# Attention over a cached window with output projection: the last output block in pieces of 512, 256, 160 and 96 columns, its last store in two row halves

## The chip, the cores and the metric

The kernel runs on one core of one Trainium2 chip. The metric is device time in microseconds, the median of several executions. One more execution was recorded with the hardware profiler; durations and times within the run come from that one.

## The reference

Queries are projected from x, attend over the last 2048 positions of a key and value cache (8 query heads share each of 4 key/value heads), and the result goes through an output projection:

```python
B, Sq, D = 8, 32, 1024
Hq, Hkv, Sk, Dh = 32, 4, 8192, 128
W = min(4096, max(256, Sk // 4))
rep = Hq // Hkv
q = (x @ wq).reshape(B, Sq, Hq, Dh).transpose(0, 2, 1, 3)
k = jnp.repeat(k_cache[:, :, Sk - W:, :], rep, axis=1)
v = jnp.repeat(v_cache[:, :, Sk - W:, :], rep, axis=1)
scores = jnp.einsum("bhqd,bhkd->bhqk", q, k) * (Dh ** -0.5)
o = jnp.einsum("bhqk,bhkd->bhqd", softmax(scores), v)
out = o.transpose(0, 2, 1, 3).reshape(B, Sq, Hq * Dh) @ wo
```

Everything is bf16. The output is 256 rows (8 batches of 32 positions) by 1024 columns, 512 KB.

## The kernel before

The work is cut into 32 units, one for each pair of batch and key/value head, ordered by head (line 129). A unit has four chunks of four key blocks; each chunk is a set of score matmuls (line 504), an exponential on ScalarE (line 506) and, two chunks later, the matmuls of probabilities with values (line 515). VectorE normalizes a finished unit and turns it into OT (`finish_unit`, lines 441 to 453), the stationary operand of the output projection. Projections of queries and of outputs are cut into small pieces which `side_plan` puts between the chunks by hand-written slots, so that TensorE always has work. The order of the instructions on each engine is the order in which the program issues them (manual schedule, line 75).

`o_pieces` (line 309) makes the output projection. For one head group g and one block t of 128 output rows it goes over column pieces given by `cuts`; each piece has four parts of two matmuls (line 322), which add up in one PSUM tile. After the fourth part VectorE takes the sum out. For the first three groups it is collected in `oacc` in FP32; for the last group it is added to `oacc`, written as bf16 to an `o_t` tile (line 332) and stored (line 334). A store goes out on SyncE's queue (SP) where its first column is 0 or 768, and else on ScalarE's (ACT).

The last group of the first row block is in the plan. The last group of the second row block is the end of the kernel: `tail_begin` (line 533) finishes the last unit, counts whether all softmax sums were in range, and makes the pieces with the cuts (512, 256, 128, 128) in line 541. `tail_mid` (line 546) runs the matmuls of the first piece and the first half of the second and opens two PSUM tiles for the last two pieces, under their first columns 768 and 896. Between the two, the engines read the count and branch: a fallback with the exact maximum, which is not taken here, or `tail_end` (line 554), which does the first piece's eviction and store, the rest of the second piece, and the last two. So the last four stores are, in order: 512 columns on SP, 256 on ACT, 128 on SP, 128 on ACT, each of 128 rows, each waiting for its eviction.

At the end of the tile context, shown by the profile as line 689, SP waits for the semaphores of all DMAs, one instruction after the other, before the engines meet in a closing barrier. The DMAs of the whole program use eight completion semaphores in turn, in the order in which they are issued in the program.

Of the kernel before, what the change touches and what calls it, by code (L numbers as in the profile page):

```python
# [108 lines left out]
class Fast:  # L109
# [199 lines left out]
    def o_pieces(self, g, t, cuts=(512, 512), st=None):  # L309

        nc, P = self.nc, self.P
        st = {} if st is None else st
        last = g == self.Hkv - 1

        def piece(n0, w, i, mm=None):

            if i == 0 and n0 not in st:
                st[n0] = self.ps_m.tile([P, 512], FP32, name="op_ps", tag="m")
            ps = st[n0]
            for k in range(i * 2, i * 2 + 2) if mm is not False else ():  # L320
                gq, c = g * self.QT_N + k // 4, k % 4
                nc.tensor.matmul(ps[:, 0:w], lhsT=self.OT[:, gq, c, t * P:(t + 1) * P],  # L322
                                 rhs=self.wo_t[gq][:, c, n0:n0 + w], start=(k == 0), stop=(k == 7))
            if i == 3 and mm is not True:
                acc = self.oacc[:, t, n0:n0 + w]
                if g == 0:
                    nc.vector.tensor_copy(out=acc, in_=ps[:, 0:w])
                elif not last:
                    nc.vector.tensor_tensor(out=acc, in0=ps[:, 0:w], in1=acc, op=ALU.add)  # L329
                else:  # L330
                    o_t = self.osb.tile([P, 512], BF16, name="o_t")
                    nc.vector.tensor_tensor(out=o_t[:, 0:w], in0=ps[:, 0:w], in1=acc, op=ALU.add)  # L332
                    eng = nc.sync if n0 in (0, 768) else nc.scalar
                    eng.dma_start(out=self.out[t * P:(t + 1) * P, n0:n0 + w], in_=o_t[:, 0:w])
        return [lambda n0=sum(cuts[:k]), w=w, i=i, **kw: piece(n0, w, i, **kw) for k, w in enumerate(cuts) for i in range(4)]


# [195 lines left out]
    def tail_begin(self):  # L533
        self.pv_last()
        for p in self.after[:-2]:
            p()
        low = self.check_all()
        for p in self.after[-2:]:
            p()
        self.open = {}  # L540
        self.last = self.o_pieces(self.Hkv - 1, 1, (512, 256, 128, 128), self.open)
        for p in self.last[:2]:
            p()
        return low

    def tail_mid(self):
        self.last[2]()
        self.last[3](mm=True)
        for p in self.last[4:6]:
            p()  # L550
        for n0 in (768, 896):
            self.open[n0] = self.ps_o.tile([self.P, 512], FP32, name="op_ps", tag="o_ps")

    def tail_end(self):
# [139 lines left out]
```

## Time and profile before

| What | Value |
|---|---|
| Median of 5 runs | 184.38 us (184.13 to 186.41) |
| The profiled execution's own time | 184.45 us |
| Its span, first to last instruction | 182.7 us |
| Busy share of PE, DVE, ACT, POOL | 98%, 69%, 74%, 49% |
| Granted TensorE clock | 0.999 |
| Output matmuls (line 322) | 144, 36.2 us busy |
| Last store, issue to landing | 1.5 us |

The span is 1.8 us shorter than the execution's own time, which also holds what lies before the first and after the last instruction. PE is the matmul row, PEld the weight loads which run beside it; DVE is VectorE, ACT ScalarE, POOL GpSimd. A "q" after an engine's name is its sequencer, which issues DMAs and waits. The issue of a DMA is short; its landing comes later, and "to landing" counts from the start of the issue until the last of its semaphore's increments. The chain of waits follows the work back from the last busy instruction; it does not follow a DMA that nobody computes with, so the time after the last eviction is to be looked for in the windows and in the records of SP.

### The profile page before, as it was taken

What the parts mean: (1) busy time and instruction counts of PE and PEld (TensorE: products, weight loads), DVE (VectorE), ACT (ScalarE), POOL (GpSimd) and SP (SyncE); (2) the same over time, 40 slices, a digit from 0 to 9 for tenths busy, and PEclk for the clock granted to TensorE, in tenths of its full rate; (3) what the DMA queues carried; (4) which work ended last, traced back from release to release, by engine and by line L of the source; (5) the groups of instructions that cost most, each with busy time, mean ns of one, the idle gap of its engine ahead of it and who ended that gap; (6) DMA issues with size and microseconds to landing.
All of it is one profiled execution on the core that took longest, in us unless ns stands there. A gap on an engine that the chain in (4) does not pass through costs nothing.

```text
span 182.7 us, 5030 instructions
## 1 busy us (share of the span) xinstructions
PE 178.3 (98%) x2041; PEld 152.3 (83%) x2041; DVE 125.6 (69%) x257; ACT 135.9 (74%) x146; POOL 89.1 (49%) x138
## 2 busy tenths in 40 slices
PE   8899999999999999999999999999999999999993
PEld 3799899999999999988787899988787788888843
DVE  0238699778977698487898655967587987554253
ACT  2218898897897888997877787888878788888800
POOL 2002565069780795935949607929606959600000
PEclk9999999999999999999999999999999999999999
DMA  5999999989999999999999999999999999970013
GB/s 187 337 410 404 228 385 375 228 278 256 369 391 252 359 266 345 369 297 316 303 377 376 399 255 275 369 241 365 256 330 266 324 303 327 212 172 0 0 34 92
DMA packets 52954, 51.73 MB, mean 283 GB/s; under 512 B 39744, under 2 KB 40256, under 8 KB 52928
## 3 DMA queue, kind: packets, MB, share of 16 engines
q1 hardware_dynamic: 52352, 50.90, 98.6%
q10 hardware_dynamic: 576, 0.49, 0.8%
q8 instruction: 16, 0.26, 0.6%
q14 instruction: 10, 0.08, 0.1%
HBM read 41.42 MB, written 0.52 MB: 230 GB/s over the span
## 4 chain that ended last, share of the span: by engine, by line
PE 86%; DMA 9%; DVE 1%; SPq 1%; issue 0%
PE o_ps L515 30%; PE s_ps L504 29%; PE op_ps L322 15%; PE q_ps L285 11%; DMA k_raw<-in_k_cache_dram 9%; SPq L168 1%; PE ql_ps L301 0%; DVE kb L259 0%; DVE kT L246 0%; DVE OT L451 0%; DVE o_sb L449 0%; SPq L347 0%; DVE o_t L332 0%; PE cnt_ps L570 0%; DVE RL_all L445 0%
## 5 line engine op out<-in xcount | busy, mean ns | idle before, releaser
L506 ACT ACTIVATE pT<-s_ps 128x1024 bf16<-128x1024 f32 x128 | 128.4, 1027 | 27.2 <-PE s_ps L504 27.0
L270 POOL TENSOR_SCALAR kTv<-kb 32x512 bf16<-32x512 bf16 x126 | 84.4, 670 | 51.0 <-DVE kb L259 31.7
L515 PE MATMUL o_ps<-va,pT 128*128 128x129 bf16 x1024 | 78.8, 220 | 0.0
L515 PEld LDWEIGHTS <-pT 128*128 128x128 bf16 x1024 | 68.5, 98 | 3.1
L504 PE MATMUL s_ps<-QT,kT 128*128 128x256 bf16 x336 | 50.4, 273 | 0.2 <-DVE kT L246 0.2
L504 PEld LDWEIGHTS <-kT 128*128 128x128 bf16 x336 | 31.8, 98 | 9.8 <-DVE kT L246 0.3
L322 PE MATMUL op_ps<-wo_sb,OT 128*128 128x512 bf16 (+2 forms) x144 | 36.2, 356 | 0.0
L259 DVE STREAM_TRANSPOSE kb<-k_raw 128x512 bf16<-128x512 bf16 x44 | 29.7, 691 | 1.9 <-DMA k_raw<-in_k_cache_dram 1.5
L285 PE MATMUL q_ps<-xT,wq_sb 128*128 128x256 bf16 x192 | 28.3, 273 | 0.0
L504 PE MATMUL s_ps<-QT,kTv 128*128 128x256 bf16 x176 | 26.4, 273 | 0.0
L439 DVE COPY va<-v_sb 128x2048 bf16<-128x2048 bf16 x30 | 25.2, 841 | 1.6 <-DMA v_sb<-in_v_cache_dram 1.3
L445 DVE RECIPROCAL RL_all<-o_ps 128x2 f32<-128x2 f32 x32 | 5.3, 164 | 26.7 <-PE o_ps L515 26.4
L268 DVE COPY kTv<-kb 32x512 bf16<-32x512 bf16 x50 | 22.7, 455 | 1.2
L504 PEld LDWEIGHTS <-kTv 128*128 128x128 bf16 x176 | 17.0, 98 | 6.1
L285 PEld LDWEIGHTS <-wq_sb 128*128 128x128 bf16 x192 | 16.9, 98 | 1.2
L451 DVE STREAM_TRANSPOSE OT<-o_sb 128x256 bf16<-128x256 bf16 x32 | 14.3, 445 | 1.1
L449 DVE TENSOR_TENSOR o_sb<-o_ps,RL_all 128x256 bf16<-128x256 f32 x32 | 13.6, 424 | 1.1
L322 PEld LDWEIGHTS <-OT 128*128 128x128 bf16 x144 | 11.3, 98 | 2.3
L437 POOL TENSOR_SCALAR va<-v_sb 128x2048 bf16<-128x2048 bf16 x2 | 3.8, 1897 | 17.6 <-DMA v_sb<-in_v_cache_dram 17.6
L288 ACT CAST QT<-q_ps 128x512 bf16<-128x512 f32 x12 | 7.0, 583 | 0.2 <-PE q_ps L285 0.2
L329 DVE TENSOR_TENSOR oacc<-op_ps,oacc 128x512 f32<-128x512 f32 x8 | 5.3, 662 | 2.0 <-PE op_ps L322 2.0
L405 PE MATMUL q_ps<-xT,wq_sb 128*128 128x256 bf16 (+1 forms) x64 | 6.0, 246 | 0.7 <-DMA wq_sb<-in_wq_dram 0.5
(35 smaller groups left out, 42.5 us busy)
## 6 DMA issues: line engine op xcount, KB each, us to landing
v_sb<-in_v_cache_dram SPq DMA_DIRECT2D x30, 512.0 KB, 6.6
wo_sb<-in_wo_dram SPq DMA_DIRECT2D x16, 512.0 KB, 6.4
wq_sb<-in_wq_dram SPq DMA_DIRECT2D x13, 512.0 KB, 6.6
k_raw<-in_k_cache_dram SPq DMA_DIRECT2D x13, 512.0 KB, 5.7
wq_sb<-in_wq_dram SPq DMA_DIRECT2D x6, 256.0 KB, 5.1
v_sb<-in_v_cache_dram SPq DMA_DIRECT2D x4, 256.0 KB, 4.6
kT<-in_k_cache_dram SPq DMA_TRANSPOSE x36, 7.1
k_raw<-in_k_cache_dram SPq DMA_DIRECT2D x2, 256.0 KB, 6.4
```

Of the source, the lines that this page charges most:

```text
L259: nc.vector.transpose(out=st["kb"][:, sl, :], in_=self.k_raw[ui][:, sl, :])
L268: nc.vector.tensor_copy(out=out, in_=in_)
L270: nc.gpsimd.tensor_scalar(out=out, in0=in_, scalar1=1.0, scalar2=1.0, op0=ALU.mult, op1=ALU.mult)
L285: nc.tensor.matmul(st[k][:, hl % 2, :], lhsT=self.wq_t[g, i][:, c % (DC // 2), hl * P:(hl + 1) * P], rhs=self.xT[:, c, :], start=(c == 0 a ...
L288: nc.scalar.copy(out=self.q_view(g)[:, :, 2 * k:2 * k + 2, :].rearrange("p b h s -> p h b s"), in_=st[k][:, :, :].rearrange("p h (b s) -> ...
L322: nc.tensor.matmul(ps[:, 0:w], lhsT=self.OT[:, gq, c, t * P:(t + 1) * P], rhs=self.wo_t[gq][:, c, n0:n0 + w], start=(k == 0), stop=(k == 7))
L439: self.nc.vector.tensor_copy(out=out, in_=in_)
L449: nc.vector.tensor_tensor(out=o_sb[:, :, :, :], in0=o_ps[:, :, 0:Dh].rearrange("p q (i c) -> p q c i", c=4), in1=rl[:, ui * QT_N:(ui + 1) ...
L451: nc.vector.transpose(out=self.OT[:, g * QT_N:(g + 1) * QT_N, :, b * self.Sq:(b + 1) * self.Sq], in_=o_sb[:, :, :, :])
L504: nc.tensor.matmul(s_ps[:, jj, :], lhsT=self.kT[ui][:, c * CJ + jj, :], rhs=q_u, start=True, stop=True)
L506: nc.scalar.activation(out=pT[:, :, :], in_=s_ps[:, :, :], func=ACT.Exp, bias=0.0, scale=self.scale)
L515: nc.tensor.matmul(o_ps[:, qt, 0:self.VW], lhsT=pT[:, jj, qt * P:(qt + 1) * P], rhs=va[:, j, 0:self.VW], start=(j == 0 and qt == 0), stop= ...
```

## The change

The last two pieces are 160 and 96 columns wide instead of 128 and 128. The 256-column store moves from ACT's queue to SP's, the first of the two narrow pieces from SP's to ACT's, and the last piece is stored by two DMAs: rows 0 to 63 on SP, rows 64 to 127 on ACT.

```diff
                     nc.vector.tensor_tensor(out=o_t[:, 0:w], in0=ps[:, 0:w], in1=acc, op=ALU.add)
-                    eng = nc.sync if n0 in (0, 768) else nc.scalar
-                    eng.dma_start(out=self.out[t * P:(t + 1) * P, n0:n0 + w], in_=o_t[:, 0:w])
+                    if n0 == 928:
+                        for p0, eng in ((0, nc.sync), (P // 2, nc.scalar)):
+                            eng.dma_start(out=self.out[t * P + p0:t * P + p0 + P // 2, n0:n0 + w], in_=o_t[p0:p0 + P // 2, 0:w])
+                    else:
+                        eng = nc.sync if n0 == 0 or w == 256 else nc.scalar
+                        eng.dma_start(out=self.out[t * P:(t + 1) * P, n0:n0 + w], in_=o_t[:, 0:w])
...
-        self.last = self.o_pieces(self.Hkv - 1, 1, (512, 256, 128, 128), self.open)
+        self.last = self.o_pieces(self.Hkv - 1, 1, (512, 256, 160, 96), self.open)
...
-        for n0 in (768, 896):
+        for n0 in (768, 928):
             self.open[n0] = self.ps_o.tile([self.P, 512], FP32, name="op_ps", tag="o_ps")
```

After the change the last five stores are: 512 columns on SP, 256 on SP, 160 on ACT, and 96 columns by 64 rows on each of SP and ACT. Nothing else of the program is changed.

## The prediction

> **What bounds the kernel now.** I read the page first, then the chain of waits over the last microseconds, the groups by shape of the same stretch, a table of windows, and last the single records of the stores and of SyncE's (SP's) closing waits. The page's chain says where the whole time lies:
>
> ```profile
> PE 86%; DMA 9%; DVE 1%; SPq 1%; issue 0%
> ```
>
> TensorE sets the time nearly from end to end, and none of its earlier work is touched. So the question is only what follows the last matmuls. The chain of waits from 178 us on:
>
> ```profile
> 177.94 2.00 PE op_ps L322 x25
> 179.94 0.02 issue
> 179.96 0.29 DVE o_t L332
> ```
>
> It ends at 180.25 with VectorE's last eviction, but the span ends at 182.67: the last 2.42 us are store and closing, which the chain does not follow. The windows (columns: length, then busy time of PE, PEld, DVE, ACT, POOL with counts, then granted clock, DMA share, GB/s):
>
> ```profile
> 178.86:179.98 1.12, 1.06 (x18) 0.88 (x15) 0.83 (x4) 0.00 (x0) 0.00 (x0) 1.00 0.22 65
> 179.98:180.62 0.64, 0.00 (x0) 0.00 (x0) 0.27 (x1) 0.00 (x0) 0.00 (x0) 1.00 0.77 221
> 180.62:181.78 1.16, 0.00 (x0) 0.00 (x0) 0.00 (x0) 0.00 (x0) 0.00 (x0) 1.00 0.32 71
> 181.78:182.67 0.89, 0.00 (x0) 0.00 (x0) 0.00 (x0) 0.00 (x0) 0.00 (x0) 0.77 0.00 0
> ```
>
> The reader is to see four stages: 16 matmuls of 128 columns with evictions; the last eviction and the issue of the last store; 1.16 us of that store's flight with every compute engine idle; 0.89 us of closing barrier. The last two stores (issue times near 180 us), and SP's closing waits in two stretches:
>
> ```profile
> L334 SPq DMA_DIRECT2D out_dram<-o_t x1: 618/618/618, 179.8 to 179.8; - x1
> L334 ACTq DMA_DIRECT2D out_dram<-o_t x1: 339/339/339, 180.3 to 180.3; - x1
> DMA to landing us min/median/max: 1.5/1.6/1.8
> ...
> L689 SPq EVENT_SEMAPHORE  x4: 28/28/28, 180.5 to 180.7; - x4
> ...
> L689 SPq EVENT_SEMAPHORE  x4: 28/28/28, 181.3 to 181.8; - x4
> ```
>
> SP closes the program by waiting for the eight store and load semaphores one after the other. The first four were long complete and pass at 180.495, 180.564, 180.631 and 180.695: 67 ns apiece, the bare price of a wait. The other four are the last four stores in the order of their landing; they pass at 181.257, 181.445, 181.620 and 181.792, each about 16 ns after its store landed (the last at 181.776). So only the last landing is paid, and the seven other waits hide under it. From the eighth wait to the end it is 0.88 us.
>
> **The change, part by part.**
>
> *Matmuls.* 8 x 128 and 8 x 128 columns become 8 x 160 and 8 x 96, the same columns in all. In the records the starts are 55.8 ns apart at 128 columns, 109 at 256, 216 at 512: 2.5 ns plus columns at 2.4 per ns. So 160 columns take 69.3 ns. No matmul of 96 is in the trace: by the line through the rows 42.6 ns, and, if the 128-column weight load ahead of each (98 ns long, back to back at the same 56 ns) is as fast as it gets, 56. The Trainium skill (TensorE: Matmul & The Clock Gate, Back-to-back issue gap) has both sides: N/2.4 + 2.5 for a lone matmul, and about 81 ns at N=128 for a stream of load and matmul. This trace's 55.8 ns in such a stream speaks for the line; with a floor of 81 the last eight would end 0.31 us later. I take 42.6: the last matmul starts at 178.865 + 8 x 0.0693 + 7 x 0.0426 = 179.717 instead of 179.702; the 56 ns end adds 0.09 us and is kept for the range.
>
> *Evictions.* The shapes give VectorE's price and the matmul's latency:
>
> ```profile
> L332 DVE TENSOR_TENSOR o_t<-op_ps,oacc 128x512 bf16<-128x512 f32 x3 | 2.1, 692 | 3.8 <-PE op_ps L322 3.8
> L322 PE MATMUL op_ps<-wo_sb,OT 128*128 128x128 bf16 x16 | 1.1, 219 | 0.0
> L332 DVE TENSOR_TENSOR o_t<-op_ps,oacc 128x128 bf16<-128x128 f32 x2 | 0.6, 290 | 0.2 <-PE op_ps L322 0.2
> L332 DVE TENSOR_TENSOR o_t<-op_ps,oacc 128x256 bf16<-128x256 f32 x1 | 0.4, 425 | 0.1
> ```
>
> From 290 and 425 ns it is 1.05 ns a column: 160 columns cost 324, 96 cost 256. The eviction of 160 can start when its matmuls are out (179.35 + 0.23 + 0.04 = 179.62) and ends at 179.94; that of 96 starts 0.245 us after the last matmul's start (0.258 before, less 13 ns of shorter matmul), at 179.96, and ends at 180.22 instead of 180.25. The longer eviction is just hidden by TensorE; gain 0.03 us.
>
> *Stores that change queue.* The 256-column store goes from ACT to SP. SP's queue holds the 512 store (issued 178.98 to 179.33), so it is free at 179.52 and pays nothing. The 160-column store goes to ACT at 179.97 and holds ACT's queue for 0.34 us (339 to 356 ns in ACT's three rows), to 180.32. Neither is late for anybody but what stands behind them: ACT's half store. That one can only be issued at 180.32 plus about 0.09 for the wait and issue between two stores, some 180.41, where before the last store went out at 180.28. SP's half finds SP free and goes out at 180.25.
>
> *The split.* One store of 32 KB becomes two of 12 KB: one more issue, one more semaphore. A store's first packet comes 0.49 to 0.52 us after its issue ended in all six stores, and the last landing 0.66 us after the first packet for both 256-byte stores. Of those 0.66 us, eight packets per DMA engine of about 16 to 18 ns are 0.13; halving the rows saves about 0.06. The Trainium skill speaks against the split (DMA: Bandwidth & Descriptors, Rules for kernel authors): two transfers on disjoint partition halves serialize on the same 16 engines, so one should not bother. By that rule the saving is nothing, by the packets' row 0.06; I take 0.06, since the two are issued 0.16 us apart and each has only some 0.07 us of packets. The flight is a fixed latency in the main, which a half store pays in full. The time to issue 64 rows is in no row: 0.34 if fixed, 0.17 if it goes with the rows. I take 0.34, since 1024, 512 and 256 byte rows cost 349, 343 and 339, so it hardly follows size; SP's last issue, 618, is the upper end. Then SP's half lands at 180.25 + 0.34 + 0.50 + 0.60 = 181.69 and ACT's at 180.41 + 0.34 + 0.50 + 0.60 = 181.85, against 181.78 before.
>
> *The closing waits.* Here the change costs something that its lines don't show. The DMAs take eight semaphores in turn, and the last store of before had the eighth. The added store is therefore on the first one again, and the built program gives it to SP's half: the first of SP's eight closing waits now asks for that store's landing. The other seven, which passed under the flight before, stand behind it: 7 x 67 ns = 0.47 us. The eighth passes at 181.69 + 0.02 + 0.47 = 182.18 instead of 181.79. ACT's half, landing at 181.85, is hidden by that. Everything after (0.88 us) is the same.
>
> *Sum.* 182.18 - 181.79 = +0.39 us: matmul and eviction -0.03, halved store -0.06, closing waits +0.47, rounding +0.01. The profiled execution is 184.45 us, 1.78 more than its span, and would be 184.84. The median of the runs shown, 184.38, is 0.07 below it, so I forecast **184.77 us**, 0.2% more. A measurement of this kernel can tell about 1%, 1.8 us, from no change, so in these terms it is no change.
>
> **The rivals.**
>
> 1. *Issue time goes with the rows.* With 0.17 for a half store SP's lands at 181.52, the eighth wait passes at 182.01: +0.22, 184.60 us. For it: the descriptors are halved. Against it: the flat row above.
> 2. *SP's issue is long again.* The 618 ns row fell beside the other stores' packets, and SP's half, beside ACT's issues, may meet the same: 0.28 more, +0.67, 185.05 us. Its cause isn't in the profile, so I can't exclude it; three of four other late stores that overlap traffic or another issue kept to 0.35.
> 3. *It gains, with the end set by the landing of the last half.* With an issue of 0.17, ACT's half lands at 181.68, and if the closing waits cost nothing the end moves by -0.10: 184.28 us. The 67 ns steps at 180.5 to 180.7 speak against it, and so does the place of SP's half as the first wait.
> 4. *Slower by over 1%: small rows written badly.* The last rows are 192 bytes, starting 1856 bytes into a 2048-byte row of the output. If such a write takes much longer to be confirmed than the 256-byte one, everything waits for it. It decides from 1.84 - 0.39 = 1.45 us more, 2.1 us instead of 0.66 from first packet to landing; at that price the time is 186.2 us. Against it: packets of 1024, 512 and 256 bytes took 46, 27 and 18 ns, a smooth row, and 256 bytes showed no step.
>
> **How the numbers follow.** The forecast 0.54, rival 1 0.17, rival 2 0.16, rival 3 0.1, rival 4 0.03. The likeliest one's own range is 184.5 to 185.0. The range over all adds rival 2 with the weight-load bound on top (185.05 + 0.09) and a share of the scatter of the five runs (184.13 to 186.41, above the median more than below), and rival 3 with it below: 184.2 to 185.4. Faster by over 1% needs 1.8 us out of 2.4 that are nearly all fixed latency: 0.01. Slower by over 1% is rival 4 and a disturbed median: 0.04. Within 1%: 0.95.
>
> **What would show it.** Right: a first closing wait that passes near 181.7 and seven behind it at 67 ns steps, the eighth near 182.2; ACT's half issued near 180.4; last matmuls 43 ns apart; span near 183.1. Wrong: closing waits that end with the last landing (rival 3), an SP issue well above 0.34 (rival 2) or near 0.17 (rival 1), matmuls of 96 columns at 56 ns (0.09 more), or over a microsecond from packet to landing (rival 4).

## The result and the profile after

The changed kernel is slower by 0.42%: the ratio of its time to the kernel before is 1.0042, 95% interval 1.0028 to 1.0055. Its median is 185.5 us (42 runs) against 184.69 us for the kernel before in 79 runs. The forecast was 184.77 us, +0.39, in a range that ended at 185.4. The direction was right, the cost was twice as large, and the result lies just above the range. A part of the miss is the base: with more runs the median before moved from 184.38 to 184.69. But the difference itself, 0.8 us, is also twice the forecast.

The profiled execution took 185.34 us, its span went from 182.7 to 183.6. Of this 0.9 us, 0.21 lie ahead of everything that was changed: the eviction of the 512-column piece starts at 178.475 us instead of 178.263, with the same program up to there. Such scatter comes from run to run (over all traces of this case that start lies between 178.00 and 178.74). So all times below that are called "from the mark" are counted from the start of that eviction, in the single records of each trace. There the eighth closing wait passes at 3.53 us before and at 4.21 after: the change costs 0.68 us in the tail.

The chain of waits of the changed kernel from 178.2 us on ends in the same way as before:

```profile
178.15 2.00 PE op_ps L322 x25
180.15 0.02 issue
180.17 0.26 DVE o_t L332
```

The same 2.00 us of matmuls, and an eviction of 0.26 instead of 0.29. The windows of the changed kernel, cut at the same events as before (first of the last 16 matmuls, start of the last eviction, end of the last store's issue, 0.01 us ahead of the eighth closing wait, end; columns as in the windows of before):

```profile
179.08:180.17 1.09, 1.05 (x18) 0.91 (x15) 0.84 (x3) 0.00 (x0) 0.00 (x0) 1.00 0.15 45
180.17:181.17 1.00, 0.00 (x0) 0.00 (x0) 0.26 (x1) 0.00 (x0) 0.00 (x0) 1.00 0.62 186
181.17:182.67 1.50, 0.00 (x0) 0.00 (x0) 0.00 (x0) 0.00 (x0) 0.00 (x0) 1.00 0.17 31
182.67:183.56 0.89, 0.00 (x0) 0.00 (x0) 0.00 (x0) 0.00 (x0) 0.00 (x0) 0.62 0.00 0
```

The compute stage became no longer (1.09 for 1.12) and the closing barrier is the same (0.89). The two stages between them grew: eviction and issue from 0.64 to 1.00, flight and closing waits from 1.16 to 1.50. The shapes of the last pieces in the changed kernel:

```profile
L322 PE MATMUL op_ps<-wo_sb,OT 128*128 128x160 bf16 x8 | 0.7, 233 | 0.0
L322 PE MATMUL op_ps<-wo_sb,OT 128*128 128x96 bf16 x8 | 0.5, 206 | 0.0
...
L332 DVE TENSOR_TENSOR o_t<-op_ps,oacc 128x160 bf16<-128x160 f32 x1 | 0.3, 325 | 0.1
L332 DVE TENSOR_TENSOR o_t<-op_ps,oacc 128x96 bf16<-128x96 f32 x1 | 0.3, 256 | 0.0
```

The two half stores, SP's and ACT's (columns: shortest, median and longest time of the issue, then when it started):

```profile
L335 SPq DMA_DIRECT2D out_dram<-o_t x1: 562/562/562, 180.5 to 180.5; - x1
...
L335 ACTq DMA_DIRECT2D out_dram<-o_t x1: 544/544/544, 180.6 to 180.6; - x1
...
DMA to landing us min/median/max: 1.8/1.8/1.9
```

Both issues are over 0.54 us long, where the last store of before took 339 ns, and both need 1.8 to 1.9 us to land instead of 1.5. SP's closing waits in the changed kernel:

```profile
L693 SPq EVENT_SEMAPHORE  x8: 27/28/28, 182.2 to 182.7; - x8
```

All eight now stand in one row from 182.240 to 182.682; before, they were spread from 180.5 to 181.8, and the last one alone was open when the last store landed.

### The profile page after: what moved, and what is told of

Same layout as the page of the kernel before. It is cut to its first block, busy times and chain, and to the rows that moved or that the text cites. A ratio compares the mean times of both kernels' runs of the same rounds, so it can differ in the third digit from the quotient of the medians.

```text
span 183.6 us, 5032 instructions
## 1 busy us (share of the span) xinstructions
PE 178.3 (97%) x2041; PEld 152.4 (83%) x2041; DVE 126.1 (69%) x257; ACT 136.0 (74%) x146; POOL 89.0 (48%) x138
## 4 chain that ended last, share of the span: by engine, by line
PE 88%; POOL 4%; DMA 3%; SPq 1%; issue 1%; DVE 0%
PE o_ps L519 30%; PE s_ps L508 29%; PE op_ps L322 15%; PE q_ps L285 10%; POOL kTv L270 4%; DMA wq_sb<-in_wq_dram 3%; PE q_ps L409 2%; PE ql_ps L301 1%; PE tp L244 1%; SPq L168 1%; PE kf_ps L401 0%; SPq L351 0%; DVE o_t L332 0%; PE cnt_ps L574 0%
## 5 line engine op out<-in xcount | busy, mean ns | idle before, releaser
L322 PE MATMUL op_ps<-wo_sb,OT 128*128 128x512 bf16 (+3 forms) x144 | 36.2, 356 | 0.0
```

## The experiments

Three theories were to be told apart. *W*: the first closing wait asks for a late store, so seven waits run open behind it. *H*: the halves themselves are dear, because both queues issue at once (called C further on) or because of their 64 rows (R). *N*: the narrow rows, 192 bytes at byte 1856, are dear. The verdicts on these theories rest mainly on the records of one trace for each kernel; the times can tell a kernel from the one before, but not two changed kernels a tenth of a microsecond apart.

**The 96-column piece stored whole.**

```diff
-                    if n0 == 928:
-                        for p0, eng in ((0, nc.sync), (P // 2, nc.scalar)):
...
+                    eng = nc.sync if n0 in (0, 928) or w == 256 else nc.scalar
+                    eng.dma_start(out=self.out[t * P:(t + 1) * P, n0:n0 + w], in_=o_t[:, 0:w])
```

> The changed kernel, but the 96-column piece is stored whole, by one DMA of 128 rows on SP. Times are counted from the start of the eviction of the 512-column piece, so that what varies earlier drops out: there the eighth closing wait passes at 3.53 us in the kernel before and at 4.21 in the changed one. Theory H (halves: a store of 64 rows, or two issued at once, is dearer to issue and starts later): issue 0.34 us, first packet 0.50 after it, landing near 3.45, eighth wait near 3.47, tail 0.05 shorter than before. Theory N (rows of 192 bytes at byte 1856 are what is dear): issue near 0.55, first packet 0.64 to 0.76 after it, landing near 3.8, tail 0.3 longer than before. In time: H 184.6 us against 184.7 for the kernel before, N 185.0.

Measured: ratio to the kernel before 1.0011 (0.9994 to 1.0028). The store of the piece in this kernel, beside the 160-column one:

```profile
L334 ACTq DMA_DIRECT2D out_dram<-o_t x1: 342/342/342, 180.0 to 180.0; - x1
L334 SPq DMA_DIRECT2D out_dram<-o_t x1: 332/332/332, 180.2 to 180.2; - x1
```

332 ns for rows of 192 bytes, first packet 0.50 us after the issue ended, landing 3.41 and eighth wait 3.43 us from the mark: 0.10 less than before. N falls, and so does the last rival of the forecast. The pieces of 160 and 96 columns with their new queues end a tenth of a microsecond earlier in this trace, which the times can't show. All the loss belongs to the split.

**The split and the new queues, with pieces of 128 and 128.**

```diff
-                    if n0 == 928:
+                    if n0 == 896:
...
-        self.last = self.o_pieces(self.Hkv - 1, 1, (512, 256, 160, 96), self.open)
+        self.last = self.o_pieces(self.Hkv - 1, 1, (512, 256, 128, 128), self.open)
...
-        for n0 in (768, 928):
+        for n0 in (768, 896):
```

> The changed kernel with its queues and its split, but with the last pieces 128 and 128 columns wide again: the halves are 64 rows of 256 bytes. Theory H: as in the changed kernel, issues near 0.55 us, first packets 0.64 to 0.76 after them, eighth wait at 4.2 to 4.3 from the eviction of the 512-column piece. Theory N: issues 0.34, first packets 0.50 after, SP's half lands near 3.46, then the seven waits behind it, eighth wait near 3.93. In time: H 185.4, N 185.1, against 184.7 before.

Measured: 1.0034 (1.0010 to 1.0058). The two half stores:

```profile
L335 SPq DMA_DIRECT2D out_dram<-o_t x1: 562/562/562, 180.2 to 180.2; - x1
L335 ACTq DMA_DIRECT2D out_dram<-o_t x1: 572/572/572, 180.3 to 180.3; - x1
```

SP's first packet came 0.64 us after its issue ended, the eighth wait at 4.26 us from the mark. That is H: rows of 256 bytes pay the same as rows of 192.

**The semaphores shifted by one, after and before.** In the changed kernel one value load fewer, in the kernel before one more:

```diff
-V_HALVES = 30
+V_HALVES = 31
```

> The changed kernel, with one value load fewer (unit 30's values come in one DMA, not two), so that the eight semaphores are shifted by one and the two half stores are on the seventh and eighth of the closing waits. Theory W (the first closing wait is the last but one landing, so seven waits run open behind it): the first six waits pass under the flight, the eighth comes about 0.08 us after ACT's half lands, 4.10 instead of 4.21 from the eviction of the 512-column piece, about 0.1 us gained. Rival (the halves' landing alone sets the end): no difference, 4.2.

```diff
-V_HALVES = 30
+V_HALVES = 29
```

> The kernel before, with one value load more (unit 29's values come in two DMAs), so that its last store has the first of the eight semaphores. Its stores are untouched. Theory W: the last store lands near 3.51 us from the eviction of the 512-column piece as before, the first closing wait passes there and the eighth 7 x 63 to 67 ns later, at 3.96 to 4.00 instead of 3.53; 0.44 us more, about 185.1 us against 184.7. Rival (the closing waits cost nothing): 3.53, no difference.

Measured: the changed kernel with the shift 1.0036 (1.0016 to 1.0056), which the times can't tell from the 1.0042 without it. In its trace six closing waits pass ahead of the halves' landing, and two after it:

```profile
L693 SPq EVENT_SEMAPHORE  x6: 28/28/28, 181.3 to 182.0; - x6
...
L693 SPq EVENT_SEMAPHORE  x2: 28/28/28, 182.8 to 182.8; - x2
```

The eighth passes at 4.11 us from the mark, as W had it. The kernel before with the shift: 1.0035 (1.0016 to 1.0053). Its last store was issued as before (339 ns) and landed at 3.485, and the closing waits ran from 3.50 to 3.94 us from the mark. In this trace the eight stand in a row again:

```profile
L689 SPq EVENT_SEMAPHORE  x8: 28/28/28, 182.0 to 182.5; - x8
```

So the kernel before, with the shift, shows the price of the order of waits by itself: 0.44 us for seven waits behind a late first one, of which 0.41 remain from eighth wait to eighth wait, as the store landed 0.03 earlier. In the changed kernel the order costs only the last tenth: ACT's half lands at 4.02, so with the best order the end is still at 4.11 instead of 3.53.

**SP's half alone** (ACT's half left out).

```diff
-                        for p0, eng in ((0, nc.sync), (P // 2, nc.scalar)):
-                            eng.dma_start(out=self.out[t * P + p0:t * P + p0 + P // 2, n0:n0 + w], in_=o_t[p0:p0 + P // 2, 0:w])
+                        nc.sync.dma_start(out=self.out[t * P:t * P + P // 2, n0:n0 + w], in_=o_t[0:P // 2, 0:w])
```

> The changed kernel, with ACT's half store left out: rows 64 to 127 of the last 96 columns are not written. SP's half is issued with no other queue issuing, apart from the last 0.07 us of the 160-column store's issue. Theory C (both queues issuing at once makes an issue long): issue 0.33 to 0.35 us, first packet 0.50 after it. Theory R (a store of 64 rows is itself dearer): 0.56 and 0.64, exactly as in the changed kernel.

Measured, in one profiled execution; the half store in this kernel:

```profile
L334 SPq DMA_DIRECT2D out_dram<-o_t x1: 561/561/561, 180.1 to 180.1; - x1
```

561 ns, and 0.64 us from its end to the first packet, with no other queue issuing but for the first 0.07 us. C falls for the half that SP stores.

**Halves by columns.**

```diff
-                        for p0, eng in ((0, nc.sync), (P // 2, nc.scalar)):
-                            eng.dma_start(out=self.out[t * P + p0:t * P + p0 + P // 2, n0:n0 + w], in_=o_t[p0:p0 + P // 2, 0:w])
+                        for c0, eng in ((0, nc.sync), (w // 2, nc.scalar)):
+                            eng.dma_start(out=self.out[t * P:(t + 1) * P, n0 + c0:n0 + c0 + w // 2], in_=o_t[:, c0:c0 + w // 2])
```

> The changed kernel, but the last piece is split by columns: 48 columns of all 128 rows on SP, 48 on ACT, issued at the same times as the row halves were. Theory C: both issues 0.5 us and more, first packets 0.6 to 0.8 after, SP's lands near 3.75 us from the eviction of the 512-column piece. Theory R: issues 0.33 to 0.35, first packets 0.50 after; SP's store lands near 3.40, ACT's near 3.58, and the eighth closing wait passes 0.46 after SP's landing, at 3.86 instead of 4.21; in time 0.35 us less than the changed kernel, 0.3 more than the kernel before.

Measured: 1.0035 (1.0015 to 1.0055). Its two stores:

```profile
L335 SPq DMA_DIRECT2D out_dram<-o_t x1: 332/332/332, 180.3 to 180.3; - x1
...
L335 ACTq DMA_DIRECT2D out_dram<-o_t x1: 385/385/385, 180.5 to 180.5; - x1
DMA to landing us min/median/max: 1.4/1.5/1.5
```

Each of them holds the 12 KB that a row half holds. So neither the bytes nor two queues issuing side by side make the row halves dear: the second issue is some 45 ns longer, not 200, and both first packets come 0.50 us after. The first closing wait passes at 3.44 and the eighth at 3.88 us from the mark, as R and W together said (3.86).

**Other row counts.** The same split with rows 0 to 95 and 96 to 127, then 80 and 48, then three stores of 32, 64 and 32:

```diff
-                        for p0, eng in ((0, nc.sync), (P // 2, nc.scalar)):
+                        for p0, p1, eng in ((0, 96, nc.sync), (96, P, nc.scalar)):
...
```

> The changed kernel, with the last piece split into rows 0 to 95 on SP and 96 to 127 on ACT. Theory R: every count of rows under 128 is dearer; whether 96 and 32 rows cost the same as 64 (a step: 0.56 us and 0.64) or more the fewer they are is open. Theory C: both near 0.55, as they are issued side by side like the row halves.

```diff
...
+                        for p0, p1, eng in ((0, 80, nc.sync), (80, P, nc.scalar)):
...
```

> The changed kernel, with the last piece split into rows 0 to 79 on SP and 80 to 127 on ACT. Theory S (a store of exactly 64 rows is dear): issues 0.35 to 0.39 us, first packets 0.50 after, as with 96 and 32 rows. Theory M (stores near the middle sizes are dear, 32 and 96 lie outside): issues near 0.5 and first packets later than 0.6.

```diff
...
+                        for p0, p1, eng in ((0, 32, nc.sync), (32, 96, nc.scalar), (96, P, nc.sync)):
...
```

> The changed kernel, with the last piece in three stores: rows 0 to 31 on SP, 32 to 95 on ACT, 96 to 127 on SP. Theory S: ACT's store of 64 rows costs 0.54 us of issue and 0.76 to its first packet though it starts at row 32, SP's two of 32 rows 0.35 and 0.50. Rival P (only a store of an exact half of the partitions, starting at 0 or 64, is dear): all three near 0.35 and 0.50.

The records of one execution of each show it. The stores of 96 (SP) and 32 rows (ACT):

```profile
L335 SPq DMA_DIRECT2D out_dram<-o_t x1: 347/347/347, 180.4 to 180.4; - x1
...
L335 ACTq DMA_DIRECT2D out_dram<-o_t x1: 383/383/383, 180.6 to 180.6; - x1
```

and those of the three-way split, two of 32 rows on SP and one of 64, from row 32 on, on ACT:

```profile
L335 SPq DMA_DIRECT2D out_dram<-o_t x2: 345/381/417, 180.4 to 180.8; - x2
...
L335 ACTq DMA_DIRECT2D out_dram<-o_t x1: 634/634/634, 180.5 to 180.5; - x1
```

With 80 and 48 rows the issues were 380 and 402 ns and the first packets 0.50 and 0.57 us after. So R in its wide form, that fewer rows than 128 are dearer, falls as well: stores of 32, 48, 80, 96 and 128 rows in the last place cost 0.33 to 0.42 us, and only those of 64 rows 0.54 to 0.63, from whichever row they start (0, 32 or 64). P (an exact half, from row 0 or 64) and M (the middle counts) fall.

S (exactly 64 rows) holds for the issue, but not for every first packet. A 64-row store that stands alone or first has its first packet 0.64 us after its issue ended, the other row counts 0.50 to 0.57, with one exception that S did not foresee: the third store of the three-way split, 32 rows on SP issued 0.23 us after the 64 rows on ACT, had its first packet only 0.74 us after a 0.42 us issue. The second half stores of the changed kernel and of the two kernels like it, too, have 0.76 to 0.90. So a store close behind one of 64 rows was late in all four kernels that have one, whatever its own rows.

The 80-row store also went out late, at 2.15 instead of 1.98 us from the mark, since SP was still issuing the 256-column store (799 ns; on this, see the last section).

**The split without either surcharge**: rows 96 and 32, and the shift of the semaphores.

```diff
-V_HALVES = 30
+V_HALVES = 31
...
+                        for p0, p1, eng in ((0, 96, nc.sync), (96, P, nc.scalar)):
...
```

> The split with neither surcharge: rows 96 and 32, and one value load fewer (unit 30's values in one DMA), so that the two stores are on the seventh and eighth closing waits. Theory W and the records of the 96 and 32 row split: ACT's store lands at 3.59 us from the eviction of the 512-column piece, the eighth wait passes at 3.67, against 4.21 in the changed kernel, 3.53 before and 3.43 with the last piece stored whole; some 0.14 us slower than before, 184.9 against 184.7. Rival (halving the rows does gain once the surcharges are gone): under 3.43.

Measured: 1.0003 (0.9980 to 1.0026), no difference that can be told; the eighth wait at 3.75 us from the mark, ACT's store landing at 3.67. In the records it is 0.22 later than before and 0.32 later than the piece stored whole. It is also 0.08 later than expected: the 256-column store had a 629 ns issue and landed at 3.16, and the three stores behind it landed in steps of 0.17, at 3.33, 3.50 and 3.67. In the same split without the shift, where that issue took 347 ns, ACT's store landed at 3.59. Nothing was found in which the split gains.

Four of the kernels differ, apart from scatter, in the two surcharges alone. Their eighth waits pass at 3.75 us from the mark with neither (3.67 if the 0.08 is taken off), 3.87 with the bad order of waits alone (rows 96 and 32 without the shift), 4.11 with the 64 rows alone, and 4.21 with both. So the 64 rows are worth 0.34 to 0.44 us and the order 0.10 to 0.20. What is left, 0.24 to 0.32 above the piece stored whole (3.43), is the price of a second store as such.

## Why the prediction was wrong in its size

The direction, the place and the mechanism of the closing waits were right. The step that failed is the price of a half store: the forecast gave 64 rows the issue time and the delay to the first packet that it had read from stores of 128 rows. Both terms were mis-sized.

- *Matmuls and evictions.* Right. In the records the starts are 69.3 ns apart at 160 columns and 42.6 at 96 (0.298 us over seven), so the weight load did not set a floor, and the stream figure of the Trainium skill (TensorE: Matmul & The Clock Gate, Back-to-back issue gap), 81 ns at 128 columns, does not hold here (55.8 ns before). The evictions took 325 and 256 ns (324 and 256 foreseen).
- *Queues.* Right. SP's half was issued at 1.98 us from the mark and ACT's at 2.15, where the forecast, on the same count, had 1.99 and 2.15.
- *The issue of a half store.* Here the sum failed: "I take 0.34, since 1024, 512 and 256 byte rows cost 349, 343 and 339, so it hardly follows size". These three rows differ in the width of a row and say nothing of the count of rows. It was 0.562 on SP, +0.22, and 0.544 on ACT. The upper end, 0.62, was nearly its size, but for another reason: the 618 ns row was that of a 128-row store and had its first packet 0.49 us after, the 64-row stores have 0.64.
- *Issue to first packet.* "0.49 to 0.52 us after its issue ended in all six stores" was carried over to a shape that is not among the six: 0.642 for SP's half, +0.145, and 0.759 for ACT's, +0.26.
- *Packets to landing.* 0.56 (0.60 foreseen). The 0.66 from which the forecast started was a little too long for a flight by itself: the store ahead landed only 0.173 us earlier, and in the kernel before with the shift, where it had landed long before, the same store took 0.63.
- *Closing waits.* Right in mechanism and length: the first passed 17 ns after SP's half landed, and seven waits took 0.44 us (0.47 foreseen). But ACT's half landed at 4.02 us from the mark instead of 3.59, so it hid most of this row, and a better order would have saved only 0.10.
- *Rival 2.* Its sum, +0.67, is nearly the 0.68 measured, by luck. It expected a long issue from other stores' packets or issues beside it, and left the first packet where it was. SP's half alone and the halves by columns show that this is not the cause.

From eighth wait to eighth wait, along SP's half: issue +0.223, first packet +0.145, packets to landing -0.096, earlier issue of SP's half -0.037, waits +0.443, in all +0.678. Forecast: 0, 0, -0.06, -0.03, +0.47. The two terms that the forecast set to zero are the 0.37 us that its sum lacks; the other three together came out 0.07 lower than foreseen. The costs overlap: ACT's half, landing at 4.02, would hold the end at 4.03 without any waits behind SP's.

The Trainium skill's rule on disjoint partition halves (DMA: Bandwidth & Descriptors, Rules for kernel authors) pointed the right way, and the runs show more than it says: not only is nothing gained, the form of the half itself is charged. What stays open is why 64 rows are dear; the profile shows a longer issue and a later first packet, but not what happens in them. Instruction loading is not seen beside it: no packet of the instruction queues (q8, q14) was in flight when any of the 64-row stores was issued. The two 64-row stores of one kernel have their first packets and their landings 0.27 to 0.28 us apart, both where they were issued 0.17 apart (the changed kernel) and where it was 0.004 (pieces of 128). It looks as if something between issue and first packet took turns, which would also fit the late 32-row store; no run separated that.

## What to carry to other kernels

A store that is on the path at the very end is almost all fixed latency (here 0.34 of issue, 0.50 to the first packet, 0.6 to the landing), so making it smaller gains little. Each further store landed at least 0.17 us after the one ahead of it; it also adds a wait and can change which wait comes last: look at the order in which the program waits for its DMAs at its end, and let the last store have the last wait. A term taken from rows of the trace holds for the axis along which those rows differ; when the change moves along another axis (rows instead of columns), the term is unknown and its upper end belongs into the forecast's range with its full weight.

## What was not expected of the hardware

- A store of 64 rows took 0.54 to 0.63 us to issue and 0.64 us or more from there to its first packet, in all five kernels that have one; stores of 32, 48, 80, 96 and 128 rows in the same place took 0.33 to 0.42 and 0.50 to 0.57, but for one of 32 rows close behind one of 64 (0.74).
- In none of the twelve traces did two stores of the tail land less than 0.167 us apart, and in 19 of 45 neighbouring pairs it was 0.167 to 0.187, whatever their sizes and queues. The 16 increments of one store's semaphore are themselves spread over 0.15 us or more. So a further store at the very end lands, as far as these traces go, at least 0.167 us after the one ahead, and in the last experiment one late landing seems to have pushed back those behind it. This is read from the records; no run was made for it.
- The second store on SP's queue in the tail (before: the third piece) took 0.33 to 0.38 us in the five traces in which no 16 KB packet of the instruction queue q8 was in flight at its start, and 0.47 to 0.80 in the seven in which one was. In the kernel before such a packet ran from 0.81 to 1.80 us from the mark and SP's issue, begun at 1.57, took 618 ns; ACT's issue at 1.26, inside the same packet, took 343. It is an association only, and no run tried it. It lay off the path except where it delayed the issue of a later store (rows 80 and 48) or its landing (rows 96 and 32 with the shift).
